# Whole-tile loads for odd head pairs, and a new hand-written order, in a fused attention and MLP kernel

## The chip, the cores and the metric

The kernel runs on one core of one Trainium2 chip. The metric is the device time of one execution in microseconds (us). A core has five engines that run side by side, each working through its own instruction list in order: TensorE (PE, matrix products; its weight loads are shown apart as PEld), VectorE (DVE), ScalarE (ACT), GpSimd (POOL) and SyncE (SP), which here issues every DMA. An instruction waits on semaphores for what it needs, and everything behind it on the same engine waits with it.

## The reference

Two stages follow each other. Attention runs over 4 batches of 8 heads, 1152 positions of 64 numbers; queries are averaged in neighbouring pairs, so 576 remain. Its output, laid out as 2304 rows of 512, goes through an MLP with 2048 inner columns.

```python
q_pool = q.reshape(B, H, S // 2, 2, D).mean(axis=3)
scores = (1 / sqrt(D)) * q_pool @ k^T
scores = scores - max(scores, axis=-1)
attn = exp(scores) / (sum(exp(scores)) + 1e-9)
x = (attn @ v)  laid out as [B * 576, 512]
h = x @ w_in            # 512 -> 2048
out = (h * 1 / (1 + exp(-h))) @ w_out   # 2048 -> 512
```

## The kernel before, in words

**Split numbers.** Every 32-bit operand of a product is split in two 16-bit parts, hi and lo, and each product is made as three: hi by hi, hi by lo, lo by hi. A split costs a cast (hi) and a subtraction (lo). The two may stand on different engines: the cast on ACT or DVE, the subtraction on POOL or DVE. The two weight matrices arrive as 64-bit integers and are first rebuilt into 32-bit numbers by some six instructions for each 128 by 512 piece (lines 462 to 516).

**Tiles and jobs.** Heads are taken two at a time: a pair p fills the 128 partitions, head one in the low 64 and head two in the high 64. There are 16 pairs, 4 to a batch. A job j takes 128 queries of both heads of a pair (18 score products, two "sides"). The last 64 queries of two neighbouring pairs make a half job (36 smaller score products), so that a batch has 18 jobs and the kernel 72. A job runs: scores into PSUM (S, line 565); row maxima on DVE (nm, line 612) and their scaling (line 619); exponential on ACT with the row sums (p, line 628); hi and lo parts (phl, lines 312 or 316, and 327); two DMA transposes for each side (pt, line 651); the product with v (po, line 710, 54 matmuls); and multiplication by one over the sum (x, lines 592, 601, 756). In jobs 0 to 3 one side is transposed by PE instead (pp, line 665). When a chunk of 128 rows of x is whole it is transposed (px, line 781), split (xt) and becomes an MLP block: 4 groups of 48 first products (mm, line 843), tanh on ACT (line 857), one multiply-add on DVE (line 864), a split into g, and 48 second products (mm, line 894). There are 18 blocks. Two PSUM buffers (tag mm) serve po, px, pp, mm and the rebuilding of weights alike. There is one pair of S buffers, so the scores of a job can start only when both exponentials of the job before are done.

**The exchange of halves.** In a half job the second pair's two heads are written to PSUM with the halves exchanged, so that all four quadrants of PE's array work at once. In the kernel before, an odd pair's q and k are loaded with the halves exchanged (lines 363 and 364: two DMAs of 64 partitions each), which puts its heads back into place.

**What sets the order.** A planner at build time (class Plan) holds a priority for each operation (PRI, PREP_LEAD and the like), a cost for it on each engine that may run it, latencies between engines (LATENCY, DMA_START), and a list of tiles with their number of buffers. It plays the program through and writes out the order in which the operations are issued on each engine, and which engine runs each cast and subtraction. WAIT is how long an engine holds still for a more urgent operation that is about to be ready. POOL and those DVE operations that it marks with port=True are not planned at the same time. Nothing on the chip changes this order.

Of the kernel before, what the change touches and what calls it, by code (L numbers as in the profile page):

```python
# [36 lines left out]
P = 128  # L37
# [16 lines left out]
WAIT = 0.15  # L54
PREP_LEAD = 4.52
FIRST_LEAD, FIRST_STEP = 2.18, 1.0
W_FIRST, W_STEP, W2_LATER = 0.95, 0.3, 0.31
V_LATER = 2.46
PRI = dict(
    score=0.38, top=-1.29, exp=-0.46, hi=0.07, lo=0.24, turn=-2.68, flip=-0.71, flat=-1.02, sums=-0.28,  # L60
    rows=0.65, side=0.2, load=-1.03, raw=-1.12,
)
# [5 lines left out]
BOTH_BY_PE, ONE_BY_PE, EVERY = 0, 4, 99  # L68


LATENCY = {"pe": 0.25, "dve": 0.15, "act": 0.15, "pool": 0.15, "dma": 2.2}
DMA_START = 1.3
AHEAD, SWITCH, STEAL = 0.78, 1.69, 0.89
# [34 lines left out]
class Plan:  # L108
# [35 lines left out]
    def order(self):  # L144
# [54 lines left out]
        while len(order) < len(self.ops):  # L199
# [11 lines left out]
            while moved:  # L211
                moved = False
                for e in engines:
# [17 lines left out]
                    gone = op.end + (LATENCY["dma"] if e == "dma" else 0.07)  # L231
# [28 lines left out]
def tile_kernel(tc, q, k, v, w_in, w_out, out):  # L260
    nc = tc.nc
    with ExitStack() as ctx:
# [18 lines left out]
        pool("slots", BUFS["slots"], ["KH", "KL", "QH", "QL", "V"])  # L281
# [26 lines left out]
        def cast(cols, out, src, scale=None, by=("act", "dve")):  # L308
# [11 lines left out]
            ways = {"act": ("act", act_cost(cols), act), "dve": ("dve", dve_cost(cols, True), dve)}  # L320
# [31 lines left out]
        kh, kl, qh, ql, vt = {}, {}, {}, {}, {}  # L352

        def prepare(p):
# [3 lines left out]
            def load(key, src, own, swap):  # L358
                t = tile("b", "b", [P, S], F32, "ld", LOAD_ROOM if not first else 0)
# [8 lines left out]
                add("dma", 1.85, issue, pr + PRI["load"], writes=[("ld", p, key)], tiles=[t, *own])  # L368
                return t

            kh[p] = tile("slots", "KH", [P, S], F16)
            kl[p] = tile("slots", "KL", [P, S], F16)
            qh[p] = tile("slots", "QH", [P, NQ], F16)
            ql[p] = tile("slots", "QL", [P, NQ], F16)
            vt[p] = tile("slots", "V", [P, 2, NK * 2, D], F16)
            odd = p % 2 == 1
            tq = load("q", q, [qh[p], ql[p]], odd)
            tk = load("k", k, [kh[p], kl[p]], odd)
            tv = load("v", v, [vt[p]], False)
            lq, lk = ("ld", p, "q"), ("ld", p, "k")  # L380

# [3 lines left out]
            def v3():  # L385
                return tv().rearrange("p (a d) -> p a d", d=D)

            either(
                rest(NQ, q32, q32, lambda: tq()[:, NQ:], ("dve", "pool"), "tensor_add"),
                pr, writes=[lq], tiles=[tq], early=first and ADD_EARLY,  # L390
            )
            either(cast(NQ, qh[p], q32), pr, [lq], [("qh", p)], [qh[p], tq], early=first)
            either(cast(S, kh[p], tk), pr, [lk], [("kh", p)], [kh[p], tk], early=first)
            either(
                rest(NQ, ql[p], q32, qh[p], ("pool", "dve")),
                pr, [lq, ("qh", p)], [("ql", p)], [ql[p], qh[p], tq], early=first,
            )
            either(
                rest(S, kl[p], tk, kh[p], ("dve", "pool")),
                pr, [lk, ("kh", p)], [("kl", p)], [kl[p], kh[p], tk], early=first and p >= KL_EARLY,  # L400
            )
# [16 lines left out]
        def weights(n):  # L418
# [38 lines left out]
            def hi():  # L457
                return w()[:, u % 4, 0, c]

            add(  # L460
                "dma", 1.4,
                lambda: nc.sync.dma_start(
                    out=bits().bitcast(U32), in_=src[u, :, c].bitcast(U32)
                ),
# [524 lines left out]
```

## Time and profile before

| | |
|---|---|
| timed runs | 747.19 us median of 3 (746.16 to 747.85) |
| span of the profiled execution | 740.3 us (the timed runs count some 6 to 7 us around the span) |
| PE busy | 663.1 us, 90% |
| DVE busy | 550.2 us, 74% |
| ACT busy | 506.7 us, 68% |
| POOL busy | 324.7 us, 44% |
| DMA, mean share of 16 engines | 95%, 181 GB/s |
| PE, 40 slices, tenths | 2565678879999899999999998999899999999997 |

A digit of the last row is the busy share of a slice of 18.5 us. PE is partly idle for the first nine slices and nearly full after that; the last three slices hold MLP work only. For the profiled execution only the span was kept, so the changes below are worked out against 740.3 us and carried over to the median.

### The profile page before, as it was taken

The numbers are of one execution on the slowest core, as the hardware profiler recorded it, in microseconds if no ns is written. First come the engines' busy times: TensorE is split into PE (matmuls) and PEld (weight loads), VectorE is DVE, ScalarE is ACT, GpSimd is POOL, SyncE is SP. The second block draws the span as 40 slices with busy tenths as digits, with TensorE's granted clock in tenths as the row PEclk, the third lists the DMA queues.
The fourth block names the chain that finished last, engine by engine and source line by source line (L and its number), as shares of the span: only waits on it lengthen the run. The fifth ranks groups of instructions, "written<-read, shape, count | busy, mean of one in ns | idle before, by whom it ended". The sixth has DMA issues, their size and how long they took to land. (4 is left out here: it accounts for less than half of the span.)

```text
span 740.3 us, 23593 instructions
## 1 busy us (share of the span) xinstructions
PE 663.1 (90%) x10188; PEld 478.4 (65%) x10188; DVE 550.2 (74%) x919; ACT 506.7 (68%) x730; POOL 324.7 (44%) x196
## 2 busy tenths in 40 slices
PE   2565678879999899999999998999899999999997
PEld 1343556466766586767677676686767676858764
DVE  4798999887978777778788776788867888875110
ACT  5899987877657566759677665687848575765221
POOL 4756788877344051308561514033637151332111
PEclk9887799999999999999999999999999999999999
DMA  9989999999999989999999997999997999997000
GB/s 299 249 256 238 216 140 249 232 219 175 216 248 186 178 160 162 156 182 204 242 221 179 183 164 128 147 183 224 203 247 160 167 164 175 144 172 121 16 15 15
DMA packets 346024, 133.93 MB, mean 181 GB/s; under 512 B 333376, under 2 KB 333376, under 8 KB 345920
## 3 DMA queue, kind: packets, MB, share of 16 engines
q1 hardware_dynamic: 345920, 132.43, 94.1%
q8 instruction: 79, 1.29, 0.7%
q14 instruction: 25, 0.20, 0.1%
HBM read 45.09 MB, written 4.72 MB: 67 GB/s over the span
## 5 line engine op out<-in xcount | busy, mean ns | idle before, releaser
L628 ACT ACTIVATE p<-S,nm 128x1152 f32<-128x1152 f32 x144 | 174.9, 1215 | 98.7 <-DVE nm L619 82.0
L327 POOL TENSOR_TENSOR phl<-p,phl 128x1152 f16<-128x1152 f32 x67 | 162.4, 2428 | 139.0 <-ACT phl L312 72.8
L843 PE MATMUL mm<-xt,w 128*128 128x128 f16 x3456 | 204.9, 219 | 10.6 <-DVE xt L802 5.6
L612 DVE TENSOR_REDUCE nm<-S 128x1 f32<-128x1152 f32 x144 | 194.3, 1350 | 16.8 <-PE S L565 16.8
L843 PEld LDWEIGHTS <-w 128*128 128x128 f16 x3456 | 195.8, 98 | 16.9 <-issue 9.3
L894 PE MATMUL mm<-w,g 128*128 128x512 f16 x864 | 198.8, 380 | 0.1
L327 POOL TENSOR_TENSOR g<-t,g 128x512 f16<-128x512 f32 x71 | 95.2, 1342 | 197.9 <-ACT g L312 186.1
L710 PE MATMUL po<-V,pt 128*128 128x64 f16 (+1 forms) x4320 | 132.8, 197 | 17.0 <-DVE r L601 5.8
L710 PEld LDWEIGHTS <-pt 128*128 128x128 f16 (+1 forms) x4320 | 127.6, 104 | 28.6 <-issue 21.7
L894 PEld LDWEIGHTS <-g 128*128 128x128 f16 x864 | 80.3, 98 | 88.8 <-DVE raw L496 0.5
L327 DVE TENSOR_TENSOR phl<-p,phl 128x1152 f16<-128x1152 f32 x73 | 102.7, 1407 | 47.1 <-ACT phl L312 45.6
L312 ACT ACTIVATE phl<-p 128x1152 f16<-128x1152 f32 x115 | 133.5, 1163 | 2.8
L565 PE MATMUL S<-KH,QH 64*128 64x512 f16 (+2 forms) x480 | 91.6, 344 | 18.4 <-ACT p L628 10.3
L565 PEld LDWEIGHTS <-QH 64*128 64x128 f16 (+1 forms) x960 | 47.6, 100 | 74.2 <-issue 36.1
L565 PE MATMUL S<-KL,QH 64*128 64x512 f16 (+2 forms) x480 | 87.5, 343 | 1.2 <-DVE KL L327 1.2
L864 DVE SCALAR_TENSOR_TENSOR t<-t,mm 128x512 f32<-128x512 f32 x72 | 49.1, 683 | 51.7 <-ACT t L857 51.3
L565 PE MATMUL S<-KH,QL 64*128 64x512 f16 (+2 forms) x480 | 80.7, 341 | 0.0
L312 ACT ACTIVATE g<-t 128x512 f16<-128x512 f32 x69 | 43.4, 628 | 26.2 <-DVE t L864 26.1
L857 ACT ACTIVATE t<-mm 128x512 f32<-128x512 f32 x72 | 42.5, 590 | 17.9 <-PE mm L843 17.8
L565 PEld LDWEIGHTS <-QL 64*128 64x128 f16 (+1 forms) x480 | 29.6, 101 | 17.5 <-issue 4.4
L327 POOL TENSOR_TENSOR QL<-ld,QH 128x576 f16<-128x576 f32 x14 | 20.1, 1435 | 39.4 <-ACT QH L312 39.4
L312 ACT ACTIVATE osb<-mm 128x512 f32<-128x512 f32 x13 | 7.7, 593 | 34.5 <-PE mm L894 33.1
(54 smaller groups left out, 478.2 us busy)
## 6 DMA issues: line engine op xcount, KB each, us to landing
ld<-v SPq DMA_DIRECT2D x16, 576.0 KB, 6.1
ld<-q SPq DMA_DIRECT2D x8, 576.0 KB, 5.2
ld<-k SPq DMA_DIRECT2D x8, 576.0 KB, 5.5
ld<-q SPq DMA_DIRECT2D x16, 288.0 KB, 5.6
ld<-k SPq DMA_DIRECT2D x16, 288.0 KB, 6.5
pt<-phl SPq DMA_TRANSPOSE x280, 3.8
wide<-w_in SPq DMA_DIRECT2D x8, 512.0 KB, 6.1
wide<-w_out SPq DMA_DIRECT2D x8, 512.0 KB, 5.3
```

The source lines that it names most:

```text
L312: nc.scalar.activation(out=out(), in_=src(), func=AF.Copy, scale=scale or 1.0)
L327: return lambda: getattr(engine, op)(out=out(), in0=a(), in1=b())
L565: nc.tensor.matmul(o[to, c], lhsT=a[pp]()[rows, s], rhs=x[pp]()[rows, c], start=n == 0, stop=n == 2,)
L612: lambda: nc.vector.tensor_reduce(out=nm(), in_=ps()[:, :S], op=ALU.max, axis=AX.X),
L628: lambda: nc.scalar.activation(out=p32(), in_=ps()[:, :S], func=AF.Exp, scale=0.0625, bias=nm(), accum_out=sm()[:, col : col + 1],),
L710: nc.tensor.matmul(o[to, keep], lhsT=pt[:, hl * NK + c, cols], rhs=vv[:, vl, 2 * c + h], start=c == 0 and hl + vl == 0, stop=c == NK - 1 a ...
L843: nc.tensor.matmul(o, lhsT=w[:, f // 2 % 4, wl, cols], rhs=moving(xl, kk), start=kk == 0 and wl + xl == 0, stop=kk == 3 and wl == 1,)
L857: lambda: nc.scalar.activation(out=t(), in_=h(), func=AF.Tanh, scale=1.0 / G_SCALE),
L864: lambda: nc.vector.scalar_tensor_tensor(out=t(), in0=t(), scalar=1.0, in1=h(), op0=ALU.add, op1=ALU.mult,),
L894: nc.tensor.matmul(o(), lhsT=g[ff // 4]()[:, gl, ff % 4], rhs=w[:, u % 4, wl, e * DM : e * DM + DM], start=ff == ffs[0] and gl + wl == 0, ...
```

## The change

Three things change. First, q and k of odd pairs are loaded like the others, one DMA of 128 partitions each; in the half jobs the exchange is made in the product with v, which reads the other half of pt's columns, and in the guard that adds 1e-9 to the sums, which moves the two halves of one column across. Second, the hi and lo parts of K (and of Q) become two halves of one tile instead of two tiles. Third, nearly all of the planner's numbers are replaced: priorities, costs and latencies. (A branch for pairs in 32 bits is added too, but F32_PAIRS is 0, so it is never taken.)

```diff
-WAIT = 0.15
+WAIT = 0.11
-    score=0.38, top=-1.29, exp=-0.46, hi=0.07, lo=0.24, turn=-2.68, flip=-0.71, ...
+    score=9.97, top=-5.21, exp=-1.09, hi=2.99, lo=1.23, turn=-1.05, flip=-27.52, ...
-MLP_EVAC, T_EVAC = 10.74, -1.84
+MLP_EVAC, T_EVAC = 5.29, -12.85
-PIECES = 4, 2
+PIECES = 4, 4
-DMA_START = 1.3
+DMA_START = 0.1
...
                 def issue():
-                    if swap:
-                        nc.sync.dma_start(out=t()[low], in_=src[p, high, :])
-                        nc.sync.dma_start(out=t()[high], in_=src[p, low, :])
-                    else:
-                        nc.sync.dma_start(out=t(), in_=src[p])
+                    nc.sync.dma_start(out=t(), in_=src[p])
...
-            return [(p, p % 2), (p, 1 - p % 2)]
+            return [(p, 0), (p, 1)]
...
             def guard():
                 for i in range(2):
-                    nc.vector.tensor_scalar_add(
-                        out=r()[:, i : i + 1], in0=sm()[:, i : i + 1], scalar1=SUM_GUARD
-                    )
+                    moves = [(slice(0, P), slice(0, P))]
+                    if ch is None and i:
+                        moves = [(low, high), (high, low)]
+                    for to, at in moves:
+                        nc.vector.tensor_scalar_add(
+                            out=r()[to, i : i + 1], in0=sm()[at, i : i + 1], scalar1=SUM_GUARD
+                        )
...
-                    "dma", 1.75,
+                    "dma", 1.42,
                     lambda h=h: nc.sync.dma_start_transpose(
...
                 if ch is None:
-                    hs, parts = (0, 1), ((low, low), (high, high))
+                    hs, parts = (0, 1), ((low, (low, high)[i]), (high, (high, low)[i]))
...
-                    "pe", 9 * pe_cost(128, 64) + 0.1,
+                    "pe", 9 * pe_cost(128, 64) + 0.03,
```

The number of instructions on PE does not change (10,188 matmuls). DVE goes from 919 to 987 instructions, of which 8 are the guard's. These kinds move most: the subtraction of g goes from 71 on POOL and 1 on DVE to 29 and 43; the subtraction of phl from 67 on POOL and 73 on DVE to 81 and 59; the cast of phl from 115 on ACT and 25 on DVE to 99 and 41. The transposes stay 280, and the loads of q, k and v go from 64 DMAs to 48.

SP's list at the start of the program, before (ld are the 32-bit tiles of q, k and v, in the order of pairs 0, 1, 2; wide holds raw weights):

```order
L366 DMA ld_103<-v 128x1152
L363 DMA ld_108<-q 64x1152
L364 DMA ld_108<-q 64x1152
L363 DMA ld_115<-k 64x1152
L364 DMA ld_115<-k 64x1152
L366 DMA ld_143<-v 128x1152
L366 DMA ld_148<-q 128x1152
L366 DMA ld_157<-k 128x1152
L366 DMA ld_169<-v 128x1152
L363 DMA ld_190<-q 64x1152
L364 DMA ld_190<-q 64x1152
L651 DMA_TRANSPOSE pt_223<-phl_171 128x9x128
```

and the same place now, from the load of k of pair 3 to the first two transposes:

```order
L381 DMA ld_169<-k 128x1152
L381 DMA ld_187<-v 128x1152
L486 DMA wide_217<-w_in 128x1024 x2
L486 DMA wide_217<-w_out 128x1024
L486 DMA wide_243<-w_in 128x1024
L486 DMA wide_217<-w_out 128x1024
L486 DMA wide_243<-w_in 128x1024
L486 DMA wide_243<-w_out 128x1024 x2
L691 DMA_TRANSPOSE pt_305<-phl_283 128x9x128
L486 DMA raw_312<-w_in 128x1024
L691 DMA_TRANSPOSE pt_305<-phl_283 128x9x128
```

The first transpose stood behind the loads of two and a half pairs; it now stands behind those of all four pairs and eight loads of weights.

ACT's list for the first job, before (QH and KH are the hi parts of q and k, p the exponential of a side):

```order
L312 ACTIVATE V_120<-ld_103 128x1152
L312 ACTIVATE KH_150<-ld_115 128x1152
L312 ACTIVATE QH_155<-ld_108 128x576
L628 ACTIVATE p_21_159,sum_160<-S_12_122,nm_146 128x1152
L628 ACTIVATE p_24_165,sum_160<-S_13_123,nm_153 128x1152
L312 ACTIVATE phl_171<-p_21_159 128x1152
```

and now:

```order
L324 ACTIVATE V_115<-ld_103 128x1152
L324 ACTIVATE K_143<-ld_112 128x1152
L324 ACTIVATE V_150<-ld_118 128x1152
L324 ACTIVATE Q_157<-ld_106 128x576
L668 ACTIVATE p_22_163,sum_164<-S_12_122,nm_148 128x1152
L668 ACTIVATE p_24_167,sum_164<-S_11_121,nm_155 128x1152
L561 ACTIVATE pt_182<-pp_171 128x512
```

The cast of v of pair 1 moved ahead of the first job's exponentials, the side that PE transposes now has its exponential first, and the cast of the other side's phl moved back, behind the next job's.

DVE's list around job 44, in the full part of the program, before (nm are row maxima, the first line of each pair is the reduction and the other its scaling):

```order
L612 TENSOR_REDUCE nm_7941<-S_892_7915 128x1
L619 TENSOR_SCALAR nm_7941<-nm_7941 128x1
L612 TENSOR_REDUCE nm_7976<-S_893_7916 128x1
L756 TENSOR_TENSOR x_879_7805<-po_7947,r_7807 128x2x64
L619 TENSOR_SCALAR nm_7976<-nm_7976 128x1
L327 TENSOR_TENSOR phl_8013<-p_898_7978,phl_8013 128x1152
```

and now, for the same job:

```order
L652 TENSOR_REDUCE nm_7961<-S_873_7935 128x1
L652 TENSOR_REDUCE nm_7969<-S_872_7934 128x1
L659 TENSOR_SCALAR nm_7961<-nm_7961 128x1
L659 TENSOR_SCALAR nm_7969<-nm_7969 128x1
L328 CAST phl_8015<-p_877_7979 128x1152
L339 TENSOR_TENSOR phl_8015<-p_877_7979,phl_8015 128x1152
```

The first side's scaling moved behind the second side's reduction. The list of before has no such place; the new list has it in 43 of 72 jobs.

## Rows read from the trace of the kernel before

**Rows 1.** Busy time of each engine (and instructions) in three stretches, TensorE's granted clock, DMA

```profile
0.00:167.00 167.00, 107.38 (x1481) 75.39 (x1482) 137.08 (x241) 138.84 (x215) 118.76 (x78) 0.90 1.01 233
167.00:736.00 569.00, 555.77 (x8711) 402.98 (x8708) 413.16 (x678) 367.58 (x516) 205.94 (x119) 0.99 0.94 167
736.00:740.30 4.30, 0.00 (x0) 0.00 (x0) 0.00 (x0) 0.26 (x1) 0.00 (x0) 0.75 0.26 61
```

**Rows 2.** What PE waited for from 167 us on: total us, times, longest

```profile
PE po L710 <- DVE t L864: 4.6, 5, 2.5
PE S L565 <- ACT p L628: 2.4, 3, 1.9
```

**Rows 3.** Timeline of the start: start, duration, instruction, idle before it and releaser

```profile
4.70 1.40 POOL L327 TENSOR_TENSOR ld<-ld 128x576 f32<-128x576 f32 x1 [3.33 <-DMA ld<-q]
8.21 1.16 ACT L312 ACTIVATE V<-ld 128x1152 f16<-128x1152 f32 x1 [0.34 <-DMA ld<-v]
10.72 1.40 POOL L327 TENSOR_TENSOR ld<-ld 128x576 f32<-128x576 f32 x1 [2.55 <-DMA ld<-q]
13.39 1.16 ACT L312 ACTIVATE KH<-ld 128x1152 f16<-128x1152 f32 x1 [4.01 <-DMA ld<-k]
16.23 1.21 ACT L628 ACTIVATE p<-S,nm 128x1152 f32<-128x1152 f32 x1
17.58 1.97 PE L665 MATMUL pp<-one,p 128*128 128x128 f32 x8 [5.50 <-ACT p L628]
19.48 0.61 PE L565 MATMUL S<-KH,QH 64*128 64x512 f16 x2
38.12 0.39 PE L565 MATMUL S<-KH,QH 64*128 64x512 f16 x2
```

**Rows 4.** DMA issues: instruction, count, KB each, median us to landing

```profile
pt<-phl SPq DMA_TRANSPOSE x280, 3.8
```

**Rows 5.** Groups by line and shape: busy us, mean ns of one, idle before

```profile
L316 DVE CAST phl<-p 128x1152 f16<-128x1152 f32 x25 | 22.1, 882 | 1.8 <-ACT p L628 1.6
L327 DVE TENSOR_TENSOR phl<-p,phl 128x1152 f16<-128x1152 f32 x73 | 102.7, 1407 | 47.1 <-ACT phl L312 45.6 <-DMA pt<-phl 1.1
L327 POOL TENSOR_TENSOR phl<-p,phl 128x1152 f16<-128x1152 f32 x67 | 162.4, 2428 | 139.0 <-ACT phl L312 72.8 <-DVE phl L316 42.8 <-DVE t L864 20.4
L327 POOL TENSOR_TENSOR g<-t,g 128x512 f16<-128x512 f32 x71 | 95.2, 1342 | 197.9 <-ACT g L312 186.1 <-DVE g L316 6.0 <-DMA ld<-q 5.8
L327 DVE TENSOR_TENSOR g<-t,g 128x512 f16<-128x512 f32 x1 | 0.9, 861 | 0.0
L318 DVE TENSOR_SCALAR mm<-raw 128x512 f32<-128x512 f32 x10 | 6.8, 690 | 0.1
L592 DVE TENSOR_SCALAR r<-sum 128x1 f32<-128x1 f32 x144 | 16.0, 145 | 14.3 <-ACT p L628 14.1
```

**Rows 6.** Pieces of the chain that ended last: start us, us, what

```profile
513.94 2.68 PE mm L843 x48
584.52 1.57 PE po L710 x54
704.12 10.36 PE mm L894 x48
```

**Rows 7.** Timeline of DVE around job 44, as rows 3

```profile
431.13 1.36 DVE L327 TENSOR_TENSOR phl<-p,phl 128x1152 f16<-128x1152 f32 x1 [0.78 <-ACT phl L312]
432.40 1.35 DVE L612 TENSOR_REDUCE nm<-S 128x1 f32<-128x1152 f32 x1
433.79 0.15 DVE L619 TENSOR_SCALAR nm<-nm 128x1 f32<-128x1 f32 x1
433.86 1.35 DVE L612 TENSOR_REDUCE nm<-S 128x1 f32<-128x1152 f32 x1
```

**Rows 8.** Timeline of DVE and POOL at 353 us, as rows 3

```profile
352.90 3.47 DVE L408 SCALAR_TENSOR_TENSOR V<-ld,V 128x1152 f16<-128x1152 f32 x1
352.67 2.48 POOL L327 TENSOR_TENSOR phl<-p,phl 128x1152 f16<-128x1152 f32 x1 [0.38 <-ACT phl L312]
```

More of the change, by code (lines that the diff above doesn't have):

```diff
@@ L52 @@
 SUM_GUARD = 1e-9 * math.exp(P_SHIFT)
-WAIT = 0.15
[L55 to L58, printed above, removed]
-PRI = dict(
-    score=0.38, top=-1.29, exp=-0.46, hi=0.07, lo=0.24, turn=-2.68, flip=-0.71, flat=-1.02, sums=-0.28,
-    rows=0.65, side=0.2, load=-1.03, raw=-1.12,
+WAIT = 0.11
+PREP_LEAD = 3.13
+FIRST_LEAD, FIRST_STEP = 4.7, 2.53
+W_FIRST, W_STEP, W2_LATER = 1.73, 0.32, 0.33
+V_LATER = 0.99
+PRI = dict(
+    score=9.97,
+    top=-5.21,
+    exp=-1.09,
+    hi=2.99,
+    lo=1.23,
+    turn=-1.05,
+    flip=-27.52,
+    flat=-2.63,
+    sums=0.04,
+    rows=-32.29,
+    side=-0.34,
+    load=-25.48,
+    raw=0.61,
 )
 EARLY, KL_EARLY, T_EARLY, WLO_EARLY, ADD_EARLY = 8, 2, False, True, True
-MLP_EVAC, T_EVAC = 10.74, -1.84
+MLP_EVAC, T_EVAC = 5.29, -12.85
 BUFS = dict(w=1, slots=4, b=12, x32=2, x4=1, xt=4, g=8, t=4, acc=2, small=6, S=1, mm=2)
 RAW_ROOM, LOAD_ROOM, P32_ROOM, PHL_ROOM = 2, 4, 1, 1
-PIECES = 4, 2
+PIECES = 4, 4
 BOTH_BY_PE, ONE_BY_PE, EVERY = 0, 4, 99
+F32_PAIRS = 0
 LATENCY = {"pe": 0.25, "dve": 0.15, "act": 0.15, "pool": 0.15, "dma": 2.2}
-DMA_START = 1.3
-AHEAD, SWITCH, STEAL = 0.78, 1.69, 0.89
+DMA_START = 0.1
+AHEAD, SWITCH, STEAL = 0.57, 0.45, 0.37
 class Tile:
@@ L230, in order @@
                         free["port"] = op.end
-                    gone = op.end + (LATENCY["dma"] if e == "dma" else 0.07)
+                    gone = op.end + LATENCY[e]
                     heapq.heappush(events, op.end)
@@ L306, in either, with cast @@
             return plan.add(options, *args, **kw)
[L308 removed]
+        def cast(cols, out, src, scale=None, by=("act", "dve"), fast=True):
             def act():
@@ L386, in v3 @@
                 return tv().rearrange("p (a d) -> p a d", d=D)
-            either(
-                rest(NQ, q32, q32, lambda: tq()[:, NQ:], ("dve", "pool"), "tensor_add"),
-                pr, writes=[lq], tiles=[tq], early=first and ADD_EARLY,
-            )
[L392 to L401, printed above, removed]
+            if p < F32_PAIRS:
+                either(
+                    rest(NQ, lambda: whole32(qt[p]), q32, lambda: tq()[:, NQ:], ("dve", "pool"), "tensor_add"),
+                    pr, [lq], [("q", p)], [tq, qt[p]], early=first and ADD_EARLY,
+                )
+            else:
+                either(
+                    rest(NQ, q32, q32, lambda: tq()[:, NQ:], ("dve", "pool"), "tensor_add"),
+                    pr, writes=[lq], tiles=[tq], early=first and ADD_EARLY,
+                )
+                either(cast(NQ, part(qt, 0), q32), pr, [lq], [("qh", p)], [qt[p], tq], early=first)
+                either(cast(S, part(kt, 0), tk), pr, [lk], [("kh", p)], [kt[p], tk], early=first)
+                either(
+                    rest(NQ, part(qt, 1), q32, part(qt, 0), ("pool", "dve")),
+                    pr, [lq, ("qh", p)], [("ql", p)], [qt[p], tq], early=first,
+                )
+                either(
+                    rest(S, part(kt, 1), tk, part(kt, 0), ("dve", "pool")),
+                    pr, [lk, ("kh", p)], [("kl", p)], [kt[p], tk], early=first and p >= KL_EARLY,
+                )
             either(
@@ L471, in weights @@
             either(
-                cast(512, t, value, 2.0**-111),
+                cast(512, t, value, 2.0**-111, fast=False),
                 pr, [("raw", *tok)], [("t", *tok)], [t, raw], port=False, early=T_EARLY,
```

72 lines of the change are left out of this document (46 added, 26 removed).

## The prediction

> **What bounds the kernel now.** I read the busy time by stretch first [rows 1]: it says where there is anything to win. From 167 to 736 us PE is busy 555.8 of 569.0 us at a granted clock of 0.99. In the 167 us before that it is busy 107.4, idle 59.6, at a clock of 0.90, while DVE is busy 137.1, ACT 138.8, POOL 118.8 and the DMA engines are full (share 1.01). Behind 736 us lie 4.3 us of last eviction and store. So the kernel has a ramp, in which five engines feed each other and none is full by itself, and a main part bounded by PE. A gain in the main part can be 13.2 us of idle PE and no more; a gain in the ramp could be several times that.
>
> Then the waits of PE in the main part [rows 2]. The largest is 4.6 us in five pieces, for PSUM buffers of the product with v; 2.4 us in three pieces go to scores that wait for an exponential of the job before. No wait for a transpose is in that list: the tiles of pt were always there in time. That is a margin which the new order may spend.
>
> **The change, part by part.** Sums are against the span of 740.3 us; the median of the timed runs is 747.2, so 6.9 us are added at the end.
>
> *Whole loads at the start.* In the timeline of the start [rows 3], POOL takes q of pair 0 at 4.70 us and ACT takes v of pair 0 at 8.21, two tiles later: 1.75 us for a whole tile. The two halves of q of pair 1 let POOL go at 10.72, 2.51 us after that v, and the two halves of k of pair 1 let ACT go at 13.39, 2.67 us later. So a tile in halves costs 0.76 to 0.92 us more of the queue, and k of pair 1 should land near 8.21 + 2 x 1.75 = 11.7 instead of 13.4. ACT, idle 4.0 us before it, uses this for the cast of v of pair 1, which lands at 13.5 and takes 1.16; q's cast adds 0.67, so the exponentials start near 15.3 where the second of before started at 16.23. PE's transposes wait for the first of the two now: 16.6 instead of 17.58 us, and the scores behind them move as much. I take -0.9 us, bounds -2.5 (the whole of the earlier landing for both tiles) and +0.5 (the cast of v delays the exponentials). Of the other 12 odd loads none is waited for in the main part, where PE is full.
>
> *Eight weight loads ahead of the first transpose.* The twelve tiles take 12 x 1.75 = 21 us of the queue from about 3 us on; eight weight loads of 512 KB take 8/9 of 1.75, that is 1.56, each, 12.4 us. A transpose behind them lands at 3 + 21 + 12.4 + 3.8 [rows 4], near 40 us. Its product stands behind the scores of job 3 now, which began at 38.1 before [rows 3], so it may wait 0 to 5 us (the second transpose of the side is queued behind one more weight load). All that PE does there hangs on it, but ACT's list is the slower one. I take +1.5.
>
> *The ramp's content.* I counted what stands in each engine's list ahead of the scores or maxima of job 17, which comes just behind the ramp. PE has 48 more first products done by then, 2.68 us [rows 6]. DVE has four casts (0.88) and two subtractions of phl (1.41) less, seven first conversions of weights (0.69) more, and small change: about +0.3. ACT has four casts of phl (1.16) more and seven conversions (near 0.63) less: about +1. (Durations of the kinds from [rows 5]; the cast on ACT takes what that of v takes in [rows 3].) At job 21 DVE has about 4 us less and ACT 1 less, but PE 2.7 less as well. So for the same DVE and ACT work the new list has 1 to 2.4 us more of PE's done. What I can't read from a list is how tightly it packs: ACT idles 28 us of the ramp's 167 [rows 1], and an order that filled a third of that would win 9 to 10 us; one that packs worse by a few pieces loses 4. I take the middle of these ends, -3, which is near what the content alone gives.
>
> *Scores in the main part.* The list of before has short stretches of work between the scores of one job and of the next: from job 18 on, twenty have under 6.0 us, by 2.68 for 48 first products, 1.57 for a product with v, 10.36 for 48 second products [rows 6]. The new list has six. That can win at most the 2.4 us of [rows 2]. I take -1.5, bounds -2.4 and +3 (the next part says why).
>
> *Scaling behind the second maximum.* Around job 44 DVE reduced one side, scaled it 0.03 us later, and reduced the other [rows 7]. In 43 of 72 jobs the new list reduces both first, so the first exponential starts 1.35 us later, the second side's at once behind it, and both end some 1 us later than before.
>
> *Less room for the transposes.* From a job's scores to its product with v the median of PE's own work falls from 16.2 to 15.3 us; from job 18 on twelve jobs have under 14.3 us, four before, and the shortage against 14.3 grows from 5.2 to 8.3 us in sum. The chain between them, with nothing in its way: two reductions 2.70, two scalings 0.30, two exponentials 2.4, a cast 1.16, a subtraction on DVE 1.41 or POOL 2.43, a transpose 3.8: 11.8 to 12.8 us [rows 3 to 5, 7]. So there is 1 to 2 us for queues. The planner used to count 5.25 us for a transpose (1.3 + 1.75 + 2.2) and counts 3.72 now; the row says 3.8. That was the margin that [rows 2] show. I take +1.5, half the growth of the shortage, since many jobs keep 17 us or more; bounds 0 and +12 (twelve jobs that each wait for one foreign operation of about 1 us).
>
> *Work moved between engines.* DVE gains 42 subtractions of g (0.69 to 0.86 each, 29 to 36 us), 16 casts of phl (14 us) and, net, some 8 us of small pieces; it loses 14 subtractions of phl (20 us). It goes from 550 to 581 to 588 us, 79% of the span. ACT loses about 35 us, POOL about 10. The cover is PE's own work: a g is needed 10 us and more after its first products in most blocks. I take 0, bounds -2 and +10. The guard's eight more instructions are 8 x 0.145 = 1.2 us of DVE in eight half jobs [rows 5], hidden likewise. The exchanged product in the half jobs has the same matmuls in other quadrants: 0. The last 4.3 us stay.
>
> The place where a page speaks against the change is the move to DVE. First the row: at 352.90 us DVE's V operation, two operands in SBUF, took 3.47 us, where a subtraction of the same size takes 1.36 [rows 7]; POOL's phl had begun at 352.67 and ended at 355.15, and DVE ended 1.22 us later [rows 8]. The Trainium skill's page "SBUF — State Buffer", section "Who interferes with whom", says that a DVE instruction with two SBUF inputs and a GpSimd one that reads SBUF exclude each other, and that the later one fully blocks. This trace agrees. The rule's price here stands among the rivals; the sum does without it, because 73 subtractions of phl, which the planner kept clear of POOL, average 1.407 [rows 5], 0.05 over that 1.36.
>
> Sum: -0.9 + 1.5 - 3 - 1.5 + 1.5 + 0 = -2.4 us, a span of 737.9 and a time of 744.8.
>
> **Rivals.**
>
> *Products wait for transposes (slower).* Place: the product with v of the twelve tight jobs of the main part. Price: 1 us each, 12 us, and 2 us for scores that wait for the later exponentials, with the ramp as it was: 740.3 + 14 + 6.9 = 761; with the ramp's -3 kept, 758, and with half the price 751. It decides once the time from scores to the last transpose is over about 13.5 us in those jobs. For it: the later scaling, the lost margin. Against it: DVE's lists put reductions ahead of more.
>
> *DVE is late (slower).* If POOL blocks the 42 subtractions for the rest of what it is doing, that is 44% of the time (324.7 of 740.3) about 0.95 us (half of a mean of 1.34 and 2.43): 0.4 x 42 = 18 us of DVE; half of it reaching PE through PSUM buffers gives 747.2 + 9 = 756. This is what the lock's rule would do if the plan didn't avoid it. For it: PE's largest wait is already for a DVE eviction [rows 2]. Against: the 0.05 us above.
>
> *No change.* The ramp is bounded by sums that stayed the same, and its pieces cancel: 747. For it: DVE's and ACT's content up to job 17 is equal within 1 us.
>
> *A tighter ramp (much faster).* The full 10 us of packing and the main part as it was: 737.
>
> **How the numbers follow.** Chances: the forecast (a gain of 1.5 to 6 us, 741 to 745.7) 0.30; the tighter ramp 0.16; no change 0.19; waits for transposes 0.25; late DVE 0.10. A measurement of this kernel can tell about 0.2%, 1.5 us, from no change. Faster by more than that is the first two, 0.46; within it 0.19; slower 0.35. The range for 8 in 10 runs from 732, past the tighter ramp, to 758, where the transposes wait in full and the ramp gains; the forecast's own range is 741 to 746.
>
> **What would show it.** In the profile after: PE's transposes of job 0 at 16 to 17 us; job 3's scores near 38 and no wait over 5 us for the first pt; PE idle in the first 167 us under 57 us; PE's waits for exponentials in the main part below 2.4 us, and any wait for a transpose in the list under 3 us in sum. The forecast is wrong if PE's idle time in the main part goes over 20 us, or if the ramp's end (the point from which PE is full) moves by more than 10 us.

## The result, and the profile after

The changed kernel took 753.35 us (median of 4 runs, 751.51 to 757.56), the kernel before 747.52 beside it (4 runs). The ratio is 1.0114, 95% interval 1.0072 to 1.0157: slower, where 744.8 us and faster had been forecast. The profiled run has a span of 749.8 us, 9.5 more than that of before; the medians lie only 5.8 apart, because the profiled execution of before was one of its shorter ones.

The same windows as [rows 1], of the changed kernel:

```profile
0.00:167.00 167.00, 108.05 (x1518) 74.56 (x1519) 131.77 (x240) 136.91 (x209) 120.27 (x78) 0.92 1.01 232
167.00:745.50 578.50, 550.74 (x8670) 400.77 (x8669) 450.95 (x748) 332.53 (x485) 192.82 (x98) 0.99 0.90 164
745.50:749.80 4.30, 0.00 (x0) 0.00 (x0) 0.00 (x0) 0.25 (x1) 0.00 (x0) 0.78 0.27 61
```

PE's idle time in the ramp is what it was: 167 - 108.05 = 59.0 us, 59.6 before. In the main part it went from 13.2 to 578.5 - 550.7 = 27.8 us. PE's busy time fell by 4.4 us in all. So 14.6 us more of waiting in the main part, less the 4.4 and 0.7 of the ramp, make the 9.5. The ramp's forecast gain is not there, and the main part's margin is gone.

What PE waited for, as [rows 2]: the first six lines from 167 us on, the last from the ramp (total us, times, longest).

```profile
PE po L750 <- DMA pt<-phl: 7.0, 10, 1.2
PE mm L883 <- DVE t L904: 5.1, 3, 3.1
PE po L750 <- DVE t L904: 4.4, 3, 3.2
PE mm L883 <- issue: 3.3, 1, 3.3
PE S L597 <- ACT p L668: 3.3, 4, 1.1
PE mm L934 <- DVE t L904: 2.7, 1, 2.7
...
PE po L750 <- DMA pt<-phl: 8.0, 6, 2.6
```

Three things are new. Products wait for transposes, 15.0 us in 16 pieces, where the kernel before had no such wait, in the ramp or behind it. Waits for DVE's evictions (t) are 12.2 us in 7 pieces from 167 us on, three of them near 3 us; before they were 5.1 us in 6, the longest 2.5. And in one piece of 3.3 us PE waits for nothing that the profile shows ("issue"). One of the long waits for DVE, in the timelines of DVE, POOL and PE at 531 us (as [rows 8]):

```profile
530.94 4.34 DVE L339 TENSOR_TENSOR g<-t,g 128x512 f16<-128x512 f32 x2
535.21 0.67 DVE L904 SCALAR_TENSOR_TENSOR t<-t,mm 128x512 f32<-128x512 f32 x1
...
530.69 1.28 POOL L339 TENSOR_TENSOR Q<-ld,Q 128x576 f16<-128x576 f32 x1
531.93 2.81 POOL L339 TENSOR_TENSOR phl<-p,phl 128x1152 f16<-128x1152 f32 x1
...
535.94 0.81 PE L883 MATMUL mm<-xt,w 128*128 128x128 f16 x9 [3.10 <-DVE t L904]
```

Two subtractions of g, about 0.7 us each when nothing is in the way (0.730 in a run below), take DVE 4.34 us. They end 0.5 us after POOL's second instruction (534.74); the eviction queued behind them comes 3 us late, and PE stands. Ahead of the gap at 568 us DVE's subtractions of Q and K took 2.94 and 3.53 us beside POOL's. Ahead of the one at 201 us the subtraction of g took 1.34 us, behind two reductions of 2.62 together, so POOL's part in that gap is small. The wait at 378 us is the one for "issue" and of another kind: it is still 2.9 to 3.2 us in the kernels below in which both other waits are nearly gone, and its cause stays open. In the groups by line and shape (as [rows 5]) the subtraction of g on DVE averages 0.894 us:

```profile
L339 DVE TENSOR_TENSOR g<-t,g 128x512 f16<-128x512 f32 x43 | 38.4, 894 | 8.5 <-ACT g L324 8.0
L339 DVE TENSOR_TENSOR K<-ld,K 128x1152 f16<-128x1152 f32 x11 | 18.6, 1689 | 8.5 <-ACT K L324 8.5
L339 POOL TENSOR_TENSOR phl<-p,phl 128x1152 f16<-128x1152 f32 x81 | 198.3, 2452 | 272.1 <-DVE phl L328 135.2 <-ACT phl L324 115.1 <-DMA pt<-phl 20.2
```

The start did what was forecast. PE's timeline, against [rows 3]: the transposes of job 0 at 16.20 (17.58 before), the scores behind them at 18.10 (19.48), job 3's scores at 36.75 (38.12). The first product with v waited for DVE, not for its transpose.

```profile
16.20 1.97 PE L705 MATMUL pp<-one,p 128*128 128x128 f32 x8 [4.19 <-ACT p L668]
18.10 2.32 PE L597 MATMUL S<-K,Q 64*128 64x512 f16 x10
...
36.75 3.06 PE L597 MATMUL S<-K,Q 64*128 64x512 f16 x18
...
43.79 2.24 PE L750 MATMUL po<-V,pt 128*128 128x64 f16 x54 [1.59 <-DVE nm L659]
```

A transpose landed after a median of 4.0 us (3.8 in [rows 4]), and one in four took over 4.8, as in the kernel before; the planner now counts 3.72.

### The profile page after: what moved, and what is told of

The parts are those of the page before. It is cut to its first block, busy times and chain, and to the rows that moved or that the text cites. A ratio compares the mean times of both kernels' runs of the same rounds, so it can differ in the third digit from the quotient of the medians.

```text
span 749.8 us, 23571 instructions
## 1 busy us (share of the span) xinstructions
PE 658.8 (88%) x10188; PEld 475.3 (63%) x10188; DVE 582.7 (78%) x987; ACT 469.7 (63%) x693; POOL 313.1 (42%) x175
## 3 DMA queue, kind: packets, MB, share of 16 engines
q8 instruction: 79, 1.29, 0.7%
## 5 line engine op out<-in xcount | busy, mean ns | idle before, releaser
L339 POOL TENSOR_TENSOR phl<-p,phl 128x1152 f16<-128x1152 f32 x81 | 198.3, 2452 | 272.1 <-DVE phl L328 135.2
L597 PE MATMUL S<-K,Q 64*128 64x512 f16 (+3 forms) x1440 | 126.0, 338 | 22.9 <-ACT p L668 14.1
L597 PEld LDWEIGHTS <-Q 64*128 64x128 f16 (+1 forms) x1440 | 60.1, 100 | 90.3 <-issue 35.4
L324 ACT ACTIVATE phl<-p 128x1152 f16<-128x1152 f32 x99 | 114.1, 1162 | 3.8 <-DMA pt<-phl 2.3
L339 DVE TENSOR_TENSOR phl<-p,phl 128x1152 f16<-128x1152 f32 x59 | 82.4, 1398 | 8.3 <-ACT phl L324 7.8
L328 DVE CAST phl<-p 128x1152 f16<-128x1152 f32 x41 | 32.1, 782 | 19.2 <-ACT p L668 16.6
L339 DVE TENSOR_TENSOR g<-t,g 128x512 f16<-128x512 f32 x43 | 38.4, 894 | 8.5 <-ACT g L324 8.0
L339 POOL TENSOR_TENSOR g<-t,g 128x512 f16<-128x512 f32 x29 | 34.1, 1176 | 17.1 <-ACT g L324 14.8
L796 DVE TENSOR_TENSOR x<-po,r 128x128 f32<-128x128 f32 x72 | 20.5, 285 | 18.1 <-PE po L750 17.8
L339 POOL TENSOR_TENSOR ld<-ld 128x576 f32<-128x576 f32 x9 | 14.9, 1658 | 41.4 <-DMA ld<-q 23.8
```

What stands on the lines that cost most here:

```text
L324: nc.scalar.activation(out=out(), in_=src(), func=AF.Copy, scale=scale or 1.0)
L328: nc.vector.tensor_copy(out=out(), in_=src())
L339: return lambda: getattr(engine, op)(out=out(), in0=a(), in1=b())
L597: nc.tensor.matmul(o[to, c], lhsT=a[rows, s], rhs=x[rows, c], start=n == 0, stop=n == len(terms) - 1,)
L796: lambda: nc.vector.tensor_tensor(out=to(), in0=po()[:, : 2 * D].rearrange("p (a d) -> p a d", a=2), in1=r().unsqueeze(2).to_broadcast([P, ...
```

## Experiments

Ratios are to the kernel before, run on the same chip, with 95% intervals. "The new order" is the changed kernel's list of operations, "the old order" the list that the planner writes with its numbers of before. M is the theory that products wait for transposes because the order leaves them too little time; L, that POOL's reading holds DVE, and DVE's evictions come late.

### The structure alone, in the old order

```diff
 # the changed kernel, with before's priorities, costs and latencies
-WAIT = 0.11
+WAIT = 0.15
-DMA_START = 0.1
+DMA_START = 1.3
 ...
```

> The kernel after with every planner number of the kernel before: only the whole loads, the exchange in the half jobs' second product and guard, and the merged K and Q tiles are left of the change. PE's list is that of before, product by product. Theory M (the new order leaves the transposes no room, so the products with v wait) and theory L (POOL blocks DVE's two-operand instructions and so delays the evictions of PSUM) both expect the time of before, ratio 0.997 to 1.003. Theory S (the structure itself costs: the exchange, the merged tiles or the loads) expects about 1.01, like the whole change.

Measured: 740.39 us, **0.9913** [0.9876, 0.9951], faster than both kernels, and the best of the kernels here that do the whole work. PE's list is that of before. So the change is two changes of opposite sign: the structure is worth -0.9%, and the new order costs 1.0114 / 0.9913 = 1.020. The windows show it against after: the same ramp, 13.1 us of idle PE in the main part instead of 27.8. A transpose lands in it after a median of 4.1 us, no sooner than in the changed kernel, and PE waits for none.

```profile
0.00:167.00 167.00, 108.15 (x1488) 75.75 (x1490) 138.08 (x242) 139.65 (x215) 118.42 (x78) 0.90 0.99 233
167.00:734.70 567.70, 554.59 (x8704) 402.24 (x8700) 414.50 (x685) 366.80 (x516) 205.13 (x119) 0.99 0.91 167
```

### Odd pairs in two loads again

```diff
-                    nc.sync.dma_start(out=t(), in_=src[p])
+                    if p % 2 and src is not v:
+                        nc.sync.dma_start(out=t()[low], in_=src[p, low, :])
+                        nc.sync.dma_start(out=t()[high], in_=src[p, high, :])
+                    else:
+                        nc.sync.dma_start(out=t(), in_=src[p])
```

> The structure alone with q and k of odd pairs loaded as two DMAs of 64 partitions again, not exchanged; all else as in the structure alone (0.991). If the 64-partition loads are what the structure saves: the time of before, 0.997 to 1.003. If they are hidden and the merged tiles or the exchange in the product do it: 0.989 to 0.994.

Measured: 746.61 us, **0.9996** [0.9975, 1.0016]. The halved loads alone give back the whole 0.9% of the structure. At the start a half of 288 KB lands 1.24 to 1.29 us after a half before it, and a whole of 576 KB 1.43 us after the whole before it. With the two tiles of pair 1 in halves, k of pair 2 lands 9.0 us after v of pair 0 instead of 7.2, so each of 16 tiles costs about 0.9 us more of the queue. In the main part ACT's waits for k differ (from 167 us on, first without and then with the halved loads; total us, times, longest):

```profile
ACT K L313 <- DMA ld<-k: 0.4, 1, 0.4
```

```profile
ACT K L313 <- DMA ld<-k: 8.2, 6, 4.5
```

ACT stands still for k there, and its exponentials behind it. But the kernel before, with halved loads too, has little of it in its (short) profiled execution:

```profile
ACT KH L312 <- DMA ld<-k: 1.9, 2, 0.9
```

That the loads cost the time is shown; by which way it reaches PE is not.

### The planner's DMA costs exchanged

```diff
-DMA_START = 0.1
+DMA_START = 1.3
-                    "dma", 1.42,
+                    "dma", 1.75,
 # in the new numbers; two more costs of loads alike; the reverse in the old numbers
```

> The kernel after, with the planner's four DMA costs of before only (a transpose counted 5.25 us from its operands to its landing instead of 3.72); planned anew by that. From job 18 on no job has under 14.3 us of PE's work between scores and product (12 in the kernel after); 41 subtractions of g and 87 of phl are on DVE. Theory M: PE's waits for transposes fall from 15 us (8.0 before 167 us, 7.0 behind) to under 3, and the ratio from 1.011 to between 0.998 and 1.004. Theory L: DVE has more two-operand work than in the kernel after, evictions are as late, ratio 1.010 or more.

> The structure alone (all planner numbers of before) with the four DMA costs of the kernel after, so a transpose is counted 3.72 us; planned anew. 26 jobs from job 18 on have under 14.3 us between scores and product, with a shortage of 30.5 us in sum (12 jobs and 8.3 us in the kernel after; 4 and 5.2 before). One subtraction of g is on DVE, as before. Theory M: waits for transposes of 10 us or more in the main part and a ratio of 1.008 to 1.02. Theory L: DVE's work is that of before, ratio 0.998 to 1.003.

Measured: 773.25 us, **1.0345** [1.0306, 1.0384], and 787.08, **1.0544** [1.0500, 1.0588]. Neither settles anything: the second ratio lies outside both forecasts, and the first meets only L's open "1.010 or more". The first does shorten the waits for transposes, from 15.0 to 2.8 us, but the planner writes another list altogether, whose ramp ends 25 us later; what PE waits for in it is mostly the exponentials:

```profile
PE S L597 <- ACT p L668: 28.8, 9, 7.6
PE po L750 <- DVE raw L520: 13.5, 4, 9.8
...
PE po L750 <- DMA pt<-phl: 2.8, 2, 1.7
```

In the second, products wait 5.4 us for transposes from 167 us on, where M expected 10 or more.

A number given to a planner that writes the whole order anew is no isolated edit. All later kernels keep an order and change what runs in it.

### Half the transposes, in both orders

```diff
-                    lambda h=h: nc.sync.dma_start_transpose(
-                        out=pt()[:, h * NK : h * NK + NK], in_=phl()[:, h]
+                    lambda h=h: h or nc.sync.dma_start_transpose(
+                        out=pt()[:, :NK], in_=phl()[:, 0]
...
-                            o[to, keep], lhsT=pt[:, hl * NK + c, cols],
+                            o[to, keep], lhsT=pt[:, hl * lo * NK + c, cols],
 # lo = 0 where the transposes are DMAs: the product reads the hi part twice
```

> The kernel after in its own order, with only the hi half of each phl transposed: the lo half's DMA is left out and the product reads hi in its place, so the result lacks the lo part of the attention weights. PE's, DVE's, ACT's and POOL's lists are unchanged. Theory M: no product waits for a transpose, 15 us of waits go, 7 to 10 us of them on the path: ratio 0.998 to 1.003. Theory L: the late evictions stay, with gaps of PE of about 3 us each at 201, 378, 536 and 568 us: ratio 1.007 to 1.011.

> The structure alone (all planner numbers of before) with only the hi half of each phl transposed, the control to the same cut in the kernel after (which gave 0.978, 20 us below the kernel after). The result lacks the lo part of the attention weights. Theory M: this order has 1.5 us more room for each transpose and PE does not wait for one in the main part, so the cut wins 0 to 4 us: ratio 0.986 to 0.992. If transposes cost in another way too (the DMA engines, or PE itself), the cut wins 10 us or more here as well: 0.978 or below.

Measured: in the new order 730.99 us, **0.9781** [0.9741, 0.9822]; in the old order 741.22, **0.9921** [0.9896, 0.9947]. The same relief is worth 3.3% of the time in the new order and nothing in the old one (0.9913 without it). The old order had room for its transposes; the new one doesn't. The relief is wide: the product waits neither for the lo part's transpose nor for the subtraction that makes it, and the DMA engines have less to do, so it doesn't tell which of these comes too late. It also gives more than the 7 to 10 us that M expected, and more than the 15.0 us of waits. Between the two profiled executions (749.8 and 728.4 us) PE's idle time falls by 3.9 us in the ramp and 9.4 in the main part, and its busy time by 8.2 (658.8 to 650.6, at a granted clock of 0.971 and 0.976); no run explains the last. With half the transposes PE waits for none, but the long waits for DVE stay (from 167 us on):

```profile
PE po L750 <- DVE t L905: 4.1, 3, 3.0
PE mm L884 <- DVE t L905: 3.8, 1, 3.8
```

### The subtractions of g back on POOL

```diff
             def on(engine):
+                engine = nc.gpsimd if back else engine
 # back=True at the subtraction of g
```

> The kernel after in its own order, with the 43 subtractions of g that it has on DVE made by POOL in the same places, as in the kernel before (71 there). Theory L in the form that the move of g to DVE is the cause: DVE loses 38 us, the gaps at 201 and 536 us go, ratio 1.000 to 1.005. If it is the lock as such and not who carries g: POOL holds the pair for 50 us more, the casts and subtractions of k and q wait as before, ratio 1.008 to 1.015.

Measured: 753.46 us, **1.0094** [1.0063, 1.0125], the changed kernel's time. So taking back the move of g to DVE, on which I had weighed the lock, wins nothing: DVE is busy 554.7 us instead of 582.7 and is held in other operations (K's 11 subtractions take 1.919 us a piece, 1.689 in the changed kernel), while POOL is busy 368.3 us instead of 313.1. Since POOL's longer work may cost what DVE's shorter list wins, this doesn't show that the move of g costs nothing.

### POOL's subtraction replaced by a fill, in both orders

```diff
+                def brief():
+                    nc.gpsimd.tensor_sub(out=out()[:, :8], in0=a()[:, :8], in1=b()[:, :8])
+                    nc.gpsimd.memset(out()[:, 8:], 0.0)
+                if fill and engine is nc.gpsimd:
+                    return brief
 # fill=True at the subtraction of phl
```

> The kernel after in its own order; POOL's 81 subtractions of phl are cut to 8 columns and the rest of each lo part is filled with zeros by a write-only instruction, so the result lacks those lo parts. DVE's, ACT's and PE's lists are unchanged. Theory L (POOL's reads hold up DVE's two-operand instructions and casts, and the evictions behind them are late): DVE's subtractions of g fall from 0.89 to near 0.70 us, the 3 us gaps of PE at 201, 378, 536 and 568 us go, and the ratio falls from 1.011 to 1.000 or below. Theory M (only the transposes' landing counts): the lo parts made by POOL come up to 1 us sooner, so part of the waits for transposes go too, but the 3 us gaps stay: 1.004 to 1.009.

> Control: the changed kernel's structure with all of the planner's numbers of before, and POOL's subtraction of phl cut to 8 columns and a fill that only writes (the lo parts are left out of the result there). Without the fill this order ran at 0.991. Theory L (the new order suffers more from POOL's hold on DVE than the old one): the fill gains less here than the 1.5% that it gained in the new order, 0.985 to 0.991. If the fill is simply less work, it gains the same 1.5%: 0.974 to 0.979.

Measured: in the new order 744.48 us, **0.9965** [0.9943, 0.9987]; in the old order 741.88, **0.9919** [0.9889, 0.9949]. Again 1.5% in the new order, nothing in the old. DVE's operations with two inputs in SBUF get shorter, though nothing on DVE was touched: g from 0.894 to 0.730 us, K from 1.689 to 1.361, and DVE's whole busy time from 582.7 to 560.2. So do the seven casts of K, which read one tile only, from 1.277 to 0.879 us.

```profile
L345 DVE TENSOR_TENSOR g<-t,g 128x512 f16<-128x512 f32 x43 | 31.3, 730 | 8.4 <-ACT g L324 7.9
L345 DVE TENSOR_TENSOR K<-ld,K 128x1152 f16<-128x1152 f32 x11 | 15.0, 1361 | 9.8 <-ACT K L324 9.8
```

One of the two long casts of K in the changed kernel, with POOL beside it (five of the seven take 0.75 us):

```profile
373.92 2.52 DVE L328 CAST K<-ld 128x1152 f16<-128x1152 f32 x1 [0.95 <-DMA ld<-k]
...
373.45 2.37 POOL L339 TENSOR_TENSOR phl<-p,phl 128x1152 f16<-128x1152 f32 x1 [2.72 <-ACT phl L324]
375.79 1.91 POOL L339 TENSOR_TENSOR ld<-ld 128x576 f32<-128x576 f32 x1
```

Between the two profiled executions (749.8 and 739.5 us) PE's idle time falls by 3.4 us only and its busy time by 6.9, at a granted clock of 0.983 instead of 0.971; executions of the kernel before alone lie between 0.962 and 0.976, so the 1.5% rests on the timed runs and not on these two profiles. The fill is also shorter than the subtraction, so POOL is done sooner; the long fill below takes that apart. The gain is not whole: PE now comes sooner to the products and waits longer for their transposes, 13.4 us in 16 pieces from 167 us on (7.0 in 10 before).

### Both reliefs in the new order, with a short and a long fill

```diff
 # half the transposes and the fill, in the new order; for the long fill also:
                     nc.gpsimd.memset(out()[:, 8:], 0.0)
+                    nc.gpsimd.memset(out()[:, 8:], 0.0)
```

> The changed kernel in its own order with both earlier relieves at once: only the hi half of phl is transposed, and POOL's subtraction of phl is cut to 8 columns and a fill that only writes, so the lo parts of the exponential do not enter the result. Theory M (all of the loss is products that wait for transposes): the halved transposes alone gave 0.978, and the fill adds nothing to it, 0.975 to 0.981. Theory M+L (transposes and POOL's hold on DVE are two separate costs): the fill takes away the 3 us gaps that were left with halved transposes, some 10 us more: 0.960 to 0.972. If the two are one (DVE late, so the transposes late), less than the sum: 0.972 to 0.978.

> The changed kernel in its own order with halved transposes, as the run with both reliefs, but POOL's subtraction of phl is 8 columns and two fills (0.24 + 1.05 + 1.05 us), so that POOL is busy for about the 2.45 us of the whole subtraction and reads next to nothing; the lo parts do not enter the result. With halved transposes alone 0.978, with the short fill 0.954. Theory L (reading from SBUF holds DVE): near the short fill, 0.952 to 0.960, and DVE's subtractions of g stay near 0.73 us. If POOL's time is what counts: near the halved transposes alone, 0.972 to 0.980. In between: both.

Measured: 713.30 us, **0.9536** [0.9505, 0.9567] with the short fill, 711.98, **0.9557** [0.9527, 0.9587] with the long one. Together they win more than the sum of 3.3% and 1.5%, below the lowest forecast for the short fill; that each had hidden a part of the other fits the longer waits for transposes with the fill alone. And POOL's time doesn't count where nothing waits for the lo parts that it makes: with the long fill it is busy 300.0 us, nearly the 313.1 of the changed kernel, and neither DVE nor PE cares. In the groups by line and shape of the long fill:

```profile
L342 POOL MEMSET phl<- 128x1144 f16 x81 | 85.1, 1051 | 4.7
L341 POOL MEMSET phl<- 128x1144 f16 x81 | 85.1, 1050 | 0.0
L340 POOL TENSOR_TENSOR phl<-p,phl 128x8 f16<-128x8 f32 x81 | 20.8, 256 | 262.2 <-ACT phl L324 106.6 <-DVE phl L328 95.1 <-issue 58.8
L346 DVE TENSOR_TENSOR g<-t,g 128x512 f16<-128x512 f32 x43 | 31.5, 733 | 8.4 <-ACT g L324 7.7
```

So it is POOL's reading that holds DVE. The Trainium skill's page "SBUF — State Buffer", section "Who interferes with whom", says that a DVE instruction with two SBUF inputs contends with a GpSimd instruction that reads SBUF, not with one that only writes it. These runs agree: 0.733 us beside writing fills, 0.890 beside readers with the transposes halved alike.

The windows of the long fill show what the new order is without its two waits: PE idle 538.0 - 530.2 = 7.9 us in the main part (3.2 of them the wait for "issue"), and 49.8 in the first 167 us, 9.1 less than after.

```profile
0.00:167.00 167.00, 117.16 (x1793) 83.81 (x1794) 142.75 (x264) 147.08 (x225) 126.93 (x138) 0.94 0.78 205
167.00:705.00 538.00, 530.15 (x8399) 386.06 (x8396) 415.32 (x724) 319.89 (x469) 173.06 (x199) 0.99 0.53 108
```

### Both reliefs in the old order

The edits are those of the short fill and of the halved transposes.

> Control: the changed kernel's structure with all of the planner's numbers of before, with halved transposes and POOL's subtraction cut to 8 columns and one fill (the lo parts do not enter the result there). Each alone gave nothing in this order (0.992 and 0.992 beside 0.991). Theory: the old order has room for both, so both together give nothing either, 0.988 to 0.992, and the new order with both (0.954) is the better one of the two once its waits are gone. If each only hid the other's cost here, the pair gains as in the new order: 0.955 to 0.975.

Measured: 739.87 us, **0.9935** [0.9911, 0.9959]: nothing. With room for its transposes and a DVE that isn't held, the new order is 4% better than the old one with the same reliefs. These kernels leave work out, so their times are no target for one that does all of it.

### Products a little later, scalings a little earlier

```diff
+        for products, out_of in moves:      # each product with v of a job
+            ...                             # up to two PE pieces that follow it
+            order[n:n] = moved              # and there it is put back
```

```diff
+        for top, scaled in follows:         # reduction, scaling
+            order.remove(scaled)
+            order.insert(order.index(top) + 1, scaled)
```

> The changed kernel in its own order, except that each product with v, with the scaling of its x, is moved back on PE behind up to two of the MLP pieces that follow it, where their group had already begun. The time from a job's scores to its product grows from a median of 15.3 to 16.0 us of PE's own work, the shortage against 14.3 us falls from 8.3 to 6.4 us; no work is left out. Theory M: a part of the waits for transposes goes, 3 to 6 us: 1.003 to 1.008. If the waits for transposes cost nothing of their own: 1.009 to 1.015. If the moved pieces block PSUM buffers instead: over 1.015.

> The changed kernel in its own order, except that on DVE each scaling of a row maximum stands right behind its own reduction, as in the list of before; no work is left out. The first exponential of a job may start 1.35 us earlier in 43 jobs, the second is as before. Theory M (the later scaling is a part of the missing margin): 1.003 to 1.008. Rival (the second side's transposes decide, and they do not come earlier): 1.009 to 1.014.

Measured: 759.53 us, **1.0168** [1.0141, 1.0195], and 753.69, **1.0085** [1.0055, 1.0114]. The later products miss what M expected: they wait less for transposes (4.1 us for 7.0 from 167 us on), but what stands behind them comes later, and scores wait twice as long for exponentials (6.8 for 3.3). Room moved in from outside this full list did not help.

```profile
PE S L598 <- ACT p L669: 6.8, 8, 1.7
...
PE po L751 <- DMA pt<-phl: 4.1, 7, 1.1
```

The earlier scalings can't be told from the changed kernel: the intervals overlap, and waits for transposes are 8.4 us in 10 pieces from 167 us on and 3.5 in 4 before (7.0 and 8.0 in the changed kernel). The later scaling is no large part of the loss.

### POOL's subtraction in pieces

```diff
+                def pieces():
+                    for at in range(0, cols, 384):      # or 192
+                        to = slice(at, at + 384)
+                        nc.gpsimd.tensor_sub(out=out()[:, to], in0=a()[:, to], in1=b()[:, to])
+                if engine is nc.gpsimd and cols == S:
+                    return pieces
```

> The changed kernel in its own order; POOL's subtractions over 1152 columns (phl, 81 times, and K, 5 times) are issued as three of 384 columns each, no work is left out. If DVE is held only for the POOL instruction that is under way, DVE waits a third as long: its subtractions of g fall from 0.894 to about 0.79 us, none is over 2 us, and of the 1.5% that the fill gained some two thirds come back, less what POOL pays for two more starts (at 0.1 to 0.25 us each): 0.999 to 1.006. If DVE does not get in between POOL's pieces: 1.010 to 1.018, with the longest DVE subtraction as before (2.9 us).

> The same with six instructions of 192 columns. Held for one instruction only: DVE's subtractions of g near 0.76 us, but POOL's subtraction of phl grows by 0.5 to 1.2 us and with it the way to the transposes, of which the new order has too little: 1.002 to 1.015. If DVE does not get in between: 1.015 to 1.03.

Measured: 752.97 us, **1.0076** [1.0046, 1.0107] with three, 763.96, **1.0214** [1.0156, 1.0272] with six. The ratio with three lies between its two forecasts and can't be told from the changed kernel's. DVE is held less with three, which fits that it gets in between: g averages 0.827 us, its longest is 1.77 (2.85 before), DVE is busy 573.1 us instead of 582.7. But a subtraction of phl takes POOL 230.2 / 81 = 2.84 us now, 3.42 in six (2.45 whole), and the transposes wait for it: products wait 17.2 us for them, 24.2 in six (15.0 before). One cost seems to be turned into the other. With six, g comes to 0.883 us again and its longest to 3.04, which I had not expected; so that shorter pieces let DVE in is not shown.

```profile
L342 POOL TENSOR_TENSOR phl<-p,phl 128x384 f16<-128x384 f32 x243 | 230.2, 976 | 251.0 <-ACT phl L324 95.9 <-issue 77.9 <-DVE phl L328 75.1
L346 DVE TENSOR_TENSOR g<-t,g 128x512 f16<-128x512 f32 x43 | 35.5, 827 | 8.4 <-ACT g L324 7.9
```

## Why the prediction was wrong

The time, 753.35 us, lies in the range, and the rival "Products wait for transposes" had named the place (751 with half its price). But the forecast was for the other side, and it failed at these steps.

- **"I take +1.5, half the growth of the shortage."** This is the step that turned the sign. I read the median's room, 15.3 us against a chain of 11.8 to 12.8, and called the difference room for queues (it is 2.5 to 3.5 us, not the 1 to 2 that I wrote). But I built the chain of medians and of undisturbed durations: one transpose in four took over 4.8 us already in the kernel before, and an operation that meets POOL's took 3.47 us for 1.36 [rows 7, 8]. PE then waits 15.0 us for transposes, 7.0 in the main part, and 8.0 in the ramp, where I had priced the first transpose alone. Halving the transposes gives 3.3%, 25 us, in the new order and nothing in the old, twice my upper bound of 12. The 10 us beyond the waits stay open.
- **"Work moved between engines ... I take 0."** Replacing POOL's reads gives 11 us alone and some 17 us with the transposes halved (0.9557 against 0.9781), and again nothing in the old order. The rival "DVE is late" had the price nearly right: 18 us of DVE and 9 of time, where the fill takes 22.5 off DVE's busy time. The rule was there and the trace had shown it [rows 8]; I dismissed it for the 0.05 us by which 73 subtractions of phl differ from an undisturbed one. That was the wrong kind to look at: phl stays nearly clear of POOL in the new order too (1.398 us on average), and what is held is g, K and Q. In the trace of before, V's 16 operations and K's 14 subtractions took 1.665 and 1.539 us on average for some 1.36, so the plan didn't keep all kinds clear (the two rows behind this item). The new list's costs count 3.72 us for transposes of 4.0, so it isn't on time, and what was planned apart meets. That last step, why the two cost more now, is argued and not shown. Putting the 42 subtractions of g back on POOL wins nothing, so their place alone doesn't explain it.

```profile
L408 DVE SCALAR_TENSOR_TENSOR V<-ld,V 128x1152 f16<-128x1152 f32 x16 | 26.6, 1665 | 1.8 <-ACT V L312 1.8
L327 DVE TENSOR_TENSOR KL<-ld,KH 128x1152 f16<-128x1152 f32 x14 | 21.5, 1539 | 8.6 <-ACT KH L312 8.6
```

- **"Of the other 12 odd loads none is waited for in the main part."** True of PE, wrong for the time: the structure wins 0.9%, about 6.5 us, where I took 0.9 us, with -2.5 at the most, and halving the loads again takes it back. I had looked at PE's waits for loads only; how the loads reach PE otherwise is not shown. This error was on the other side: it hid 6.5 of the some 15 us (2.0%) that the new order loses.
- **"The ramp's content ... -3."** The first scores of job 18 start at 191.1 us before, 190.4 with the structure alone, and 191.9 after. With both reliefs they start at 179.4 and 176.1 (short and long fill), in the old order with both at 191.6. So the new order does pack the ramp better, by even more than the 10 us of the rival "A tighter ramp"; the waits for transposes and for DVE take all of it back. I had set the gain and the loss as two rivals; both came, in one list.
- **Eight weight loads ahead of the first transpose**, +1.5: 0. The first product waited for DVE, and job 3's scores came at 36.75. A whole tile took 1.43 us of the queue and not 1.75, a weight load 1.28 and not 1.56, so the first two transposes landed at 32.9 and 36.6 us instead of near 40.
- **Scores in the main part**, -1.5: PE's waits for exponentials rose from 2.4 to 3.3 us; no gain.
- **The 6.9 us around the span**: each timed run lies some 1.7 us above its own span (751.51 and 749.8 here). The profiled execution of before was simply one of its shorter ones; later runs of it had spans of 739.6 to 751.2. The forecast doesn't suffer, since 740.3 + 6.9 is the median.

Of the signs named ahead, the start came as forecast. The ramp's idle time (59.0 us, under 57 forecast), the waits for transposes in the main part (7.0, under 3) and for exponentials (3.3, under 2.4) did not, and PE idle in the main part, 27.8 us, is over the 20 that were to show the forecast wrong.

## What to carry to other kernels

A wait that the trace doesn't show may be absent because the order pays for it. When a change lowers the costs in a plan, look for the margin that they had held, and price it with the slow quarter of the durations, not with their median. To find whether a resource binds, relieve it in both orders: what gains in one and not in the other belongs to the order and not to the resource. And a load that PE never waits for can still cost time: only a run without the change in loads shows its price.

## What the runs showed of the hardware

- Beside POOL's instructions that only write (81 x 2 fills of 1.05 us) DVE's subtractions of g take 0.733 us on average; beside those that read SBUF, 0.890. A cast with one input took 2.52 us for 0.75 beside a reading POOL.
- A transfer of 64 partitions is nearly as long as one of 128: 1.24 to 1.29 us for 288 KB, 1.43 us for 576 KB.
- The 280 transposes fill much of the DMA engines' time: with half of them the mean busy share from 167 us on falls from 0.90 to 0.53.
